# Storing the last tile of results in transfers of 64 rows in place of 32 rows

## The chip, the cores and the metric

The kernel runs on one core of one Trainium2 chip. The metric is the device time of one execution in microseconds (us), from the device's own record. Three runs of the kernel before gave 1005.03, 1005.83 and 1005.90 us, so the median is 1005.83 us and the runs lie within 0.9 us (0.09%) of each other.

A core has five engines that run side by side, each with an instruction queue of its own: PE multiplies matrices, DVE and ACT do elementwise work, POOL does too and issues transfers, and SP only issues transfers. Transfers between the on-chip memory (SBUF, 128 partitions) and the device memory (DRAM) are carried by 16 DMA engines, whichever queue issues them.

## The reference

The reference has two parts. The first is an attention without softmax: for each of 8 batches and 8 heads it forms the 64 by 64 matrix `kv` from `k` and `v`, multiplies `q` by it, and divides each row by its root mean square. The heads' results, side by side, are the 4608 by 512 input `x` of the second part, a gated feed-forward layer whose 4608 by 512 result is the output.

```python
kv = np.einsum('bhsd,bhse->bhde', k, v)
out = np.einsum('bhsd,bhde->bhse', q, kv)
rms = np.sqrt(np.mean(out * out, axis=-1, keepdims=True) + 1e-06)
x = (out / rms * g_norm).transpose(0, 2, 1, 3).reshape(B * S, H * D)    # 4608 x 512
...
gate = 1.0 / (1.0 + np.exp(-(x @ w_gate)))                              # 4608 x 1536
return gate * (x @ w_val) @ w_out                                       # 4608 x 512, float32
```

## The kernel before

The 4608 rows of `x` are worked through in 9 chunks of 512 rows (`c` from 0 to 8). A chunk goes through a first layer (gate and value) and a second layer (the product with `w_out`). From chunk 1 on both layers are computed with a recursive scheme of fewer block products: `first_layer_fast` makes 26 products for each of three parts, `second_layer_fast` makes 26 products over sums of blocks. The weight sums are kept in DRAM and loaded again for each chunk by POOL's queue. The attention of the next batches runs between the products.

The order of the work is written out by hand: every engine executes its instructions in the order in which the program issues them, and semaphores hold back an instruction until what it needs is there.

**The second layer's end.** `second_layer_fast(c, at)` runs the products in the order 0, 3, 1, 2, 6, 4, 5, 7 and on to 25. After each product `finish(i)` issues the elementwise steps that the product completes (`combine`, on DVE and ACT) and then the stores that have become possible. A chunk's result is four tiles `rows[t]` of 128 rows by 512 columns, each made of two halves of 256 columns. The table `dones` says after which product a tile is done: tile 0 after product 18, tile 1 after 22, tile 2 after 24, tile 3 after 25. In the last chunk (`c == NG - 1`, that is 8), tile 3 is stored in two halves: the second half, columns 256 to 511, after product 23, the first half, columns 0 to 255, after product 25, which is the last product of the kernel.

**The stores.** `store` writes one tile. From batch 1 on the rows of a chunk do not stand in the order of the output: row `(p, g, i)` of a batch's 576 output rows, with `p` of 32, `g` of 9 and `i` of 2, was worked on at place `i`, `g`, `p`. So 32 neighbouring partitions of a tile (`QB`) are 32 output rows which lie 18 rows apart, and the next 32 partitions are the next `g`, two output rows further on. The kernel before issues one transfer for each such group of 32 rows, four for a tile. Its pattern is 32 rows by 256 or 512 float32 on both sides. In the last chunk the transfers go alternately to SP's and ACT's queue (`ends`, line 1047), in the other chunks all to SP's.

The last three stores of the kernel therefore are: second half of tile 3 (four transfers of 32 rows by 1 KB, two on each queue), tile 2 (four of 32 rows by 2 KB), first half of tile 3 (four of 32 rows by 1 KB). After them the program waits until all transfers have landed and ends.

Of the kernel before, what the change touches and what calls it, by code (L numbers as in the profile page):

```python
# [20 lines left out]
def kernel(  # L21
# [11 lines left out]
    nc = tc.nc  # L33

    B, H, S, HD = q.shape
    T, DM = out.shape
# [14 lines left out]
    QB = 32  # L51
# [14 lines left out]
    NG = T // G  # L66
    NST = 3
    NF2 = NFT // 2
    DH = DM // 2
    NT = G // P  # L70
# [459 lines left out]
    def sg_tile():  # L530
        return sgs[next(sg_turns) % len(sgs)]

    def store(c, t, ot, cols=slice(0, DM), queues=(nc.sync,)):

        r0 = i = 0
        while r0 < P:
            b, s = divmod(G * c + P * t + r0, S)
            rows = out[S * b:S * b + S, cols]
            if b < NE // NHP:
                j, p = divmod(s, NP)  # L540
                n = min(P - r0, NP - p)
                queues[i % len(queues)].dma_start(out=rows.rearrange("(p j) d -> j p d", j=NJ)[j, p:p + n],
                                                  in_=ot[r0:r0 + n, cols])
            else:

                half, c0 = divmod(s, S // 2)
                n = QB
                queues[i % len(queues)].dma_start(
                    out=rows.rearrange("(p g i) d -> i g p d", p=QB, i=2)[half, c0 // QB],
                    in_=ot[r0:r0 + n, cols])  # L550
            r0 += n
            i += 1
# [15 lines left out]
    def at_ps():  # L568
        return psum.tile([P, NAT, 512], FP32, tag="at", name="at")
# [4 lines left out]
    def take():  # L574
        i = free.popleft()
        return i, bank(i)[:, 0:GH]
# [62 lines left out]
    for token in order.split():  # L639
        name = token.rstrip("0123456789.")  # L640
        n = [int(i) for i in token[len(name):].split(".")]
# [81 lines left out]
    def h_form(v, j):  # L723
        s_ = h_at[v]
        return h_main[j][:, s_] if s_ < 4 * NT else h_more[:, j, s_ - 4 * NT]
# [3 lines left out]
    def h_sums(j, some):  # L729
        ops = []  # L730
        for v, (x, sign, y) in list(SUMS.items())[some]:
            eng = nc.vector if j == N3 - 1 and v in ON_VECTOR else nc.gpsimd
            ops.append((eng, lambda v=v, x=x, sign=sign, y=y, eng=eng: eng.tensor_tensor(  # L733
                out=h_form(v, j), in0=h_form(x, j), in1=h_form(y, j), op=op_of(sign))))
        return ops
# [41 lines left out]
    def load_granule(g):  # L777
        if g < N_GRAN:
            n = 2 * P * len(PARTS[g % NPA])
            nc.gpsimd.dma_start(out=granule(g)[:, 0:n], in_=kept1[g // NPA % N3, g % NPA][:, 0:n])  # L780
# [35 lines left out]
    for some in places.split():  # L816
        p, names = some.split(":")
# [4 lines left out]
    for f in range(1, NFT):  # L822
        if f == NFT - 1:
            last = at_ps()
# [86 lines left out]
    def combine(o, regions, steps, mult):  # L911

        o.update({r: v[1] for r, v in regions.items()})
        for step in steps.split():
            if step[0] == "s":
                nc.scalar.activation(out=o["o" + step[1]], in_=o["o" + step[1]], func=AF.Sigmoid)  # L916
            elif "*" in step:
                x, y = step.split("*")
                mult.tensor_tensor(out=o[x], in0=o[x], in1=o[y], op=ALU.mult)  # L919
            else:  # L920
                out_, expr = step.split("=")
                if expr in regions:
                    nc.scalar.copy(out=o[out_], in_=o[expr])  # L923
                else:
                    sign = "+" if "+" in expr else "-"
                    x, y = expr.split(sign)
                    tt(out=o[out_], in0=o[x], in1=o[y], op=ALU.add if sign == "+" else ALU.subtract)  # L927

    def give_all(regions, last, i):
        for r in list(regions):  # L930
            if i == last[r]:
                give(regions.pop(r)[0])
# [60 lines left out]
    def w_raw(v):  # L993
        n, l = divmod(v, 4)
        b0 = block(l, 0)
        return w2[:, b0:b0 + NF2 - 1:2, DH * n:DH * n + DH]
# [12 lines left out]
    def ring(i):  # L1009
        i %= NR  # L1010
        return places[i]

    def load_w(i):
        if i < N_FAST * NS:
            nc.gpsimd.dma_start(out=ring(i), in_=kept3[i % NS].rearrange("p (j n) -> p j n", j=N3))
# [24 lines left out]
    def second_layer_fast(c, at):  # L1040
        o = {f"t{n}": temps[:, i, 0:DH] for i, n in enumerate((0, 1, 8, 9))}
        rows = [sg_tile() for _ in range(NT)]
        for t in range(NT):
            for n in range(2):
                o[f"o{2 * t + n}"] = rows[t][:, DH * n:DH * n + DH]
        regions, used, done = {}, {}, count()
        ends = (nc.sync, nc.scalar) if c == NG - 1 else (nc.sync,)
        first_loads = {9: 0, 10: 1, 13: 2, 23: 3}
        dones = {18: 0, 22: 1, 24: 2, 25: 3}

        def product(i, js):
            name, hv, wv, _ = PRODUCTS2[i]
            if i not in used:
                used[i] = name not in regions
                if used[i]:
                    regions[name] = take()
            ws = W_AT[wv] if c == 1 else w_raw(wv) if wv < 8 else stay[wv] if wv in STAY else ring((c - 2) * NS + STREAM.index(wv))
            for j in js:
                nc.tensor.matmul(regions[name][1], h_form(hv, j), ws[:, j], start=(used[i] and j == 0),  # L1059
                                 stop=(j == N3 - 1), skip_group_check=True)  # L1060

        def finish(i):
            _, _, wv, steps = PRODUCTS2[i]
            combine(o, regions, steps, nc.gpsimd)
            give_all(regions, LAST2, i)
            if c > 1 and wv > 7 and wv not in STAY and STREAM.index(wv) + NR < NS:
                load_w((c - 2) * NS + STREAM.index(wv) + NR)
            if c == 1:
                if i in first_loads:
                    load_granule(first_loads[i])  # L1070
            elif i == 16:
                load_granule(NPA * N3 * (c - 1) + NPA - 1)
            if i in dones:
                t = dones[i]
                store(c, t, rows[t], slice(0, DH if c == NG - 1 and t == NT - 1 else DM), ends)
            elif c == NG - 1 and i == 23:
                store(c, NT - 1, rows[NT - 1], slice(DH, DM), ends)
            for step in at.get(next(done), ()):
                step()
            sums_of_h(2)  # L1080

        for j in (1, 2):
            h_fill.extend(h_sums(j, slice(SUMS_FIRST, None)))
        on_pool = deque(step for eng, step in h_fill if eng is nc.gpsimd)

        def sums_of_h(n):
            for _ in range(n):
                if on_pool:
                    on_pool.popleft()()

        sums_of_h(2)
        for eng, step in h_fill:
            if eng is nc.vector:
                step()
        h_fill.clear()
        blocks, some = range(N3), range(N3 - 1)
        product(0, blocks)
        finish(0)
        for i in (1, 2, 6):
            product(i, some)  # L1100
        product(3, blocks)
        finish(3)
        for i in range(1, NPR):
            if i != 3:
                if i in (1, 2, 6):
                    if i == 6:
                        continue
                    product(i, (N3 - 1,))
                    finish(i)
                    if i == 2:  # L1110
                        product(6, (N3 - 1,))
                        finish(6)
                else:
                    product(i, blocks)
                    finish(i)
        load_late(c + 2)

    fill.extend(x_early)
    for t in range(G // P):
        for f in range(NFT - 2, NFT):  # L1120
            second(t, f)
            slot()
        ot = sg_tile()
        nc.scalar.copy(out=ot, in_=ps[t])
        store(0, t, ot)
# [62 lines left out]
```

## Time and profile before

| what | value |
|---|---|
| median of three runs | 1005.83 us |
| the profiled execution's own time | 1004.44 us |
| its span, first to last instruction | 1002.7 us |
| PE busy | 993.8 us (99% of the span) |
| DVE, POOL, ACT busy | 722.1, 617.5, 342.5 us |
| last instruction of DVE, the last half tile | 998.77 to 999.19 us |
| granted TensorE clock | 1.00 |
| read from DRAM, written | 160.50 MB, 25.56 MB |

Times inside the profile are microseconds from the start of the span. The profiled execution took 1.39 us less than the median of the runs, and 1.74 us of its time lies outside its span. A transfer has two times: how long its issue holds the queue that issues it, and how long it takes from the start of the issue until all its data has landed. The profile also records the packets that the 16 DMA engines move; the DMA share of a stretch is the sum of the packets' times over 16 engines, so that one engine that is busy all the time is 0.06, and packets that overlap on an engine can bring it over 1.

### The profile page before, as it was taken

How to read it: one execution, taken by the hardware profiler on the slowest of the kernel's cores; microseconds unless marked ns; L12 is line 12 of the kernel's file. 1: busy time of each engine (PE TensorE's matmuls, PEld its weight loads, DVE VectorE, ACT ScalarE, POOL GpSimd, SP SyncE). 2: the span in 40 equal slices, each digit the busy share in tenths (PEclk: the TensorE clock that was granted, in tenths of full speed). 3: DMA queues.
4: the chain of work that ended last, by engine and by line, in shares of the span. 5: the costliest groups of instructions: out<-in, count | busy, mean ns of one | idle time of the engine just before them, and what ended most of it. 6: DMA issues, size and time to landing. Idle time of an engine off the chain costs nothing.

```text
span 1002.7 us, 16624 instructions
## 1 busy us (share of the span) xinstructions
PE 993.8 (99%) x5958; PEld 815.8 (81%) x5958; DVE 722.1 (72%) x1198; ACT 342.5 (34%) x606; POOL 617.5 (62%) x988
## 2 busy tenths in 40 slices
PE   8999999999999999999999999999999999999998
PEld 7455447888888888888888888888888888888887
DVE  4989999889757756784677676866587566755672
ACT  4566332562144213530344124421342133213320
POOL 1509997798359633965186707861595449744963
PEclk9999999999999999999999999999999999999999
DMA  9995414673799568846875577755864555444514
GB/s 271 269 265 183 172 51 115 215 236 127 248 301 272 176 189 240 239 156 203 257 240 171 181 223 237 203 171 179 258 201 141 167 173 211 156 149 162 214 53 122
DMA packets 156114, 195.43 MB, mean 195 GB/s; under 512 B 84832, under 2 KB 128864, under 8 KB 156032
## 3 DMA queue, kind: packets, MB, share of 16 engines
q0 software_dynamic: 22000, 114.11, 34.4%
q1 hardware_dynamic: 126864, 78.16, 27.6%
q10 hardware_dynamic: 7168, 2.10, 0.9%
q8 instruction: 47, 0.77, 0.3%
q14 instruction: 35, 0.29, 0.1%
HBM read 160.50 MB, written 25.56 MB: 186 GB/s over the span
## 4 chain that ended last, share of the span: by engine, by line
PE 73%; POOL 2%; DMA 1%; issue 0%; SPq 0%; DVE 0%; POOLq 0%
PE mm L957 46%; PE mm L1059 24%; PE at L439 1%; POOL h L733 1%; PE at L389 1%; DMA h_more<-in_v_dram 1%; POOL w_ring L1030 0%; POOL h_more L733 0%; PE at L396 0%; SPq L134 0%; POOL w L780 0%; DVE sg L927 0%; POOLq L780 0%; POOLq L1030 0%
## 5 line engine op out<-in xcount | busy, mean ns | idle before, releaser
L957 PE MATMUL mm<-xs,w 128*128 128x256 f32 x1428 | 331.8, 380 | 0.0
L957 PEld LDWEIGHTS mm<-xs,w 128*128 128x128 f32 x1428 | 270.5, 190 | 37.1
L957 PE MATMUL mm<-xT,w 128*128 128x256 f32 x948 | 229.8, 380 | 0.0
L957 PEld LDWEIGHTS mm<-xT,w 128*128 128x128 f32 x948 | 179.5, 190 | 25.0 <-issue 0.5
L780 POOL DMA_DIRECT2D w<-kept x84 | 46.8, 557 | 189.4 <-PE mm L957 187.3
L927 DVE TENSOR_TENSOR sg<-sg,mm 128x512 f32<-128x512 f32 (+1 forms) x176 | 100.7, 599 | 85.5 <-PE mm L957 41.5
L1059 PE MATMUL mm<-w,h 128*128 128x256 f32 x630 | 143.1, 379 | 0.3 <-POOL h L733 0.3
L1059 PEld LDWEIGHTS mm<-w,h 128*128 128x128 f32 x630 | 119.6, 190 | 17.0 <-POOL h L733 0.7
L919 POOL TENSOR_TENSOR h<-h,sg 128x512 f32<-128x512 f32 x72 | 96.0, 1350 | 57.0 <-DVE h L927 31.0
L923 ACT COPY temps<-mm 128x512 f32<-128x512 f32 (+1 forms) x128 | 66.0, 538 | 186.9 <-PE mm L1059 94.7
L733 POOL TENSOR_TENSOR h<-h 128x128 f32<-128x128 f32 x216 | 112.1, 531 | 16.6 <-DVE h_more L733 13.1
L1059 PE MATMUL mm<-w,h_more 128*128 128x256 f32 x474 | 108.2, 379 | 0.0
L916 ACT ACTIVATE sg<-sg 128x512 f32<-128x512 f32 x96 | 59.7, 630 | 131.5 <-DVE sg L927 131.5
L1059 PEld LDWEIGHTS mm<-w,h_more 128*128 128x128 f32 x474 | 90.1, 190 | 12.2
L923 ACT COPY sg<-mm 128x512 f32<-128x512 f32 (+1 forms) x112 | 56.9, 510 | 86.5 <-PE mm L1059 45.0
L733 POOL TENSOR_TENSOR h_more<-h 128x128 f32<-128x128 f32 x120 | 61.6, 517 | 34.3 <-DVE h L919 30.0
L927 DVE TENSOR_TENSOR temps<-temps,mm 128x512 f32<-128x512 f32 (+1 forms) x96 | 59.4, 619 | 25.9 <-PE mm L1059 16.6
L599 PE MATMUL mm<-xT,w 128*128 128x512 f32 x176 | 77.8, 596 | 0.1
L927 DVE TENSOR_TENSOR temps<-mm,temps 128x512 f32<-128x512 f32 (+1 forms) x64 | 39.8, 622 | 50.9 <-PE mm L1059 23.6
L923 ACT COPY h<-mm 128x512 f32<-128x512 f32 x48 | 28.1, 585 | 140.4 <-PE mm L957 126.4
L927 DVE TENSOR_TENSOR sg<-mm,sg 128x512 f32<-128x512 f32 (+1 forms) x64 | 39.7, 620 | 45.1 <-PE mm L957 24.5
L599 PEld LDWEIGHTS mm<-xT,w 128*128 128x128 f32 x176 | 32.6, 190 | 39.2 <-issue 36.8
(145 smaller groups left out, 1284.2 us busy)
## 6 DMA issues: line engine op xcount, KB each, us to landing
w<-kept POOLq DMA_DIRECT2D x42, 896.0 KB, 5.7
w<-kept POOLq DMA_DIRECT2D x90, 384.0 KB, 4.6
w<-kept POOLq DMA_DIRECT2D x42, 768.0 KB, 5.5
out_dram<-sg SPq DMA_DIRECT2D x119, 64.0 KB, 1.7
h_more<-in_k_dram SPq DMA_DIRECT2D x28, 256.0 KB, 5.6
h_more<-in_v_dram SPq DMA_DIRECT2D x28, 256.0 KB, 6.5
q<-in_q_dram SPq DMA_DIRECT2D x96, 72.0 KB, 5.0
xT<-xTs SPq DMA_DIRECT2D x96, 72.0 KB, 4.4
```

Source lines behind the costliest of these rows:

```text
L389: nc.tensor.matmul(ps[HD * g:HD * g + HD, m, e], mains[2 * m + g, "k"][:, c], mains[2 * m + g, "v"][:, c], start=(e == 0 and j == 0), stop ...
L439: nc.tensor.matmul(u[HD * e:HD * e + HD, o:o + HD], qTs[HD * g:HD * g + HD, c:c + HD], kvq[HD * g:HD * g + HD, t == NSL, m, e], start=True ...
L599: nc.tensor.matmul(self.ps[i], w[("wg", "wv")[i], self.f][:, m, :], xT[self.c][:, m, :], start=(m == 0), stop=(m == NMT - 1), skip_group_c ...
L733: ops.append((eng, lambda v=v, x=x, sign=sign, y=y, eng=eng: eng.tensor_tensor(out=h_form(v, j), in0=h_form(x, j), in1=h_form(y, j), op=op ...
L780: nc.gpsimd.dma_start(out=granule(g)[:, 0:n], in_=kept1[g // NPA % N3, g % NPA][:, 0:n])
L916: nc.scalar.activation(out=o["o" + step[1]], in_=o["o" + step[1]], func=AF.Sigmoid)
L919: mult.tensor_tensor(out=o[x], in0=o[x], in1=o[y], op=ALU.mult)
L923: nc.scalar.copy(out=o[out_], in_=o[expr])
L927: tt(out=o[out_], in0=o[x], in1=o[y], op=ALU.add if sign == "+" else ALU.subtract)
L957: nc.tensor.matmul(regions[name][1][:, g], ws[:, g], xf[c][wv], start=(new and g == 0), stop=True, skip_group_check=True)
L1059: nc.tensor.matmul(regions[name][1], h_form(hv, j), ws[:, j], start=(used[i] and j == 0), stop=(j == N3 - 1), skip_group_check=True)
```

## The change

`store` gets a parameter `n_groups`, the number of 32-row groups that one transfer covers. Both stores of the last chunk's tile 3 pass 2; every other store passes 1 or leaves the default of 1. With 2, a transfer takes 64 neighbouring partitions of the tile; on the DRAM side its pattern is `[half, g:g + 2]` of the same arrangement, that is 2 groups by 32 rows by 256 columns, where the groups lie two output rows apart and the rows of a group 18 rows apart. The two dimensions cannot be merged into one. Each half of tile 3 is stored in two transfers, the first on SP's queue and the second on ACT's.

```diff
-    def store(c, t, ot, cols=slice(0, DM), queues=(nc.sync,)):
+    def store(c, t, ot, cols=slice(0, DM), queues=(nc.sync,), n_groups=1):
...
                 half, c0 = divmod(s, S // 2)
-                n = QB
+                n = QB * n_groups
+                assert n_groups == 1 or c0 + n <= S // 2
+                g = c0 // QB
                 queues[i % len(queues)].dma_start(
-                    out=rows.rearrange("(p g i) d -> i g p d", p=QB, i=2)[half, c0 // QB],
+                    out=rows.rearrange("(p g i) d -> i g p d", p=QB, i=2)[half, g:g + n_groups],
                     in_=ot[r0:r0 + n, cols])
...
-                store(c, t, rows[t], slice(0, DH if c == NG - 1 and t == NT - 1 else DM), ends)
+                last = c == NG - 1 and t == NT - 1
+                store(c, t, rows[t], slice(0, DH if last else DM), ends, 2 if last else 1)
             elif c == NG - 1 and i == 23:
-                store(c, NT - 1, rows[NT - 1], slice(DH, DM), ends)
+                store(c, NT - 1, rows[NT - 1], slice(DH, DM), ends, 2)
```

## The prediction

> **What bounds the kernel now.** I read the page first, for the engine that fills the span, then the chain that ended last, for what comes after that engine's last instruction, then the rows of the last stores, then stretches of DMA traffic, for the price of a packet.
>
> The page (busy time by engine; below it the chain that ended last):
>
> ```profile
> PE 993.8 (99%) x5958; PEld 815.8 (81%) x5958; DVE 722.1 (72%) x1198; ACT 342.5 (34%) x606; POOL 617.5 (62%) x988
> ...
> PE 73%; POOL 2%; DMA 1%; issue 0%; SPq 0%; DVE 0%; POOLq 0%
> ```
>
> PE is the bound until its last product. The change touches no instruction of PE, DVE or POOL, so only what follows that product can move. The chain in order of time, its end (start us, us, what):
>
> ```profile
> 965.06 33.69 PE mm L1059 x156
> 998.74 0.02 issue
> 998.77 0.42 DVE sg L927
> ```
>
> DVE finishes the last half tile at 999.19. The span ends at 1002.66, so a tail of 3.47 us is all that a better store could ever shorten. What fills it: the transfers still in flight, the first line below from the waits of SP's queue, the others from the issues of the stretch from 985 us on (KB each, median us from issue to landing):
>
> ```profile
> SPq L1183 <- DMA out_dram<-sg: 1.2, 1, 1.2
> ...
> out_dram<-sg ACTq DMA_DIRECT2D x6, 64.0 KB, 2.0
> out_dram<-sg SPq DMA_DIRECT2D x6, 64.0 KB, 1.8
> out_dram<-sg SPq DMA_DIRECT2D x4, 32.0 KB, 1.5
> out_dram<-sg ACTq DMA_DIRECT2D x4, 32.0 KB, 1.8
> ```
>
> The second of the two issues on each queue, in the rows of the store's line (duration ns, start us; below, time to landing):
>
> ```profile
> L548 SPq DMA_DIRECT2D out_dram<-sg x1: 495/495/495, 999.6 to 999.6; - x1
> L548 ACTq DMA_DIRECT2D out_dram<-sg x1: 442/442/442, 999.6 to 999.6; - x1
> ...
> DMA to landing us min/median/max: 1.7/1.8/1.8
> ```
>
> The first issues start at 999.22 and hold SP for 0.315 and ACT for 0.375 us; the second follow about 0.4 us later, and ACT's lands at about 1001.5. From there 1.2 us of semaphores close the program. So the tail is 0.4 us for a second issue, 1.8 us of transfer, 1.2 us of closing.
>
> DMA traffic in four stretches (us, the engines' busy time, granted clock, DMA share, GB/s; the last two columns matter):
>
> ```profile
> 84.00:86.00 2.00, 2.00 (x6) 0.82 (x5) 2.00 (x3) 0.44 (x1) 2.00 (x2) 1.00 1.07 372
> 999.90:1000.03 0.13, 0.00 (x0) 0.00 (x0) 0.00 (x0) 0.00 (x0) 0.00 (x0) 1.00 0.18 32
> 1000.03:1000.34 0.31, 0.00 (x0) 0.00 (x0) 0.00 (x0) 0.00 (x0) 0.00 (x0) 1.00 0.78 182
> 1000.00:1002.00 2.00, 0.00 (x0) 0.00 (x0) 0.00 (x0) 0.00 (x0) 0.00 (x0) 1.00 0.29 66
> ```
>
> From 84 to 86 us all traffic is packets of 1 KB (742 packets, 0.74 MB) with all engines full: 372 / 16 = 23.3 GB/s for one engine, 44 ns for 1 KB. In the tail it is 66 / (0.29 x 16) = 14.2 GB/s while busy, 72 ns for 1 KB. Data of the last store begins at 1000.03, 0.81 us after its issue, and its two first transfers, 64 packets of 1 KB, are through most of the engines 0.3 us later; one engine alone would need 64 x 44 ns = 2.8 us. So a transfer of 32 rows is spread over many engines.
>
> **The change, part by part.**
>
> *Fewer issues.* Four stores of tile 3 go from eight issues to four. On each queue the second issue of the last store falls away: the last data is asked for at 999.22 instead of 999.6, a gain of up to 0.4 us. The same issues gone after product 23 (997.4) gain nothing: the store of tile 2 behind them waits for DVE, whose step ends at 997.89, when SP and ACT are nearly free as it is (tile 2's issues start at 997.98 and 998.04; at most 0.1 us earlier).
>
> *A costlier issue.* The new transfer has a third dimension. SP's transfers of three dimensions at line 473 hold the queue for 595 ns (median) against 315 for the 32-row store. I take 0.2 us more until its data starts; bounds 0 (the issue is pipelined) and 0.3.
>
> *How the data is dealt out.* Each new transfer is 64 packets of 1 KB. This decides the sum, and no row shows it: every store of the kernel before begins with 32 rows or more on both sides, and those are spread over many engines. The new one begins with 2 on the DRAM side (2 groups by 32 rows by 256). If the work is cut along the outermost dimension, as fits all rows of before, it falls into two pieces, one for each of two engines, 32 packets each. If both dimensions are cut together, 16 engines get four packets each. I take two engines: the pattern's outer dimension has only two pieces to give, and the two cannot be merged since their steps are 2 and 18 rows.
>
> The Trainium skill, "DMA: Bandwidth & Descriptors", section "Why a DMA increments its semaphore by 16 and not by 1", states this rule: the engines used are the largest number up to 16 that divides both patterns' outermost sizes larger than one, and from SP and ACT they are the lowest-numbered. By it 64 and 2 give two engines, the same two for both queues, and the sum is the one below; no run of before has such a transfer.
>
> *The sum with two engines, both queues on the same two.* The half tile after product 23 is issued at 997.09; its data starts at 997.09 + 0.81 + 0.2 = 998.1. Each of the two engines has from it 32 packets from SP and 32 from ACT. Tile 2 adds two packets of 2 KB per transfer and engine, eight in all: from 999.10 to 999.30 the traffic is 205 GB/s at a share of 0.91, 14.1 GB/s and 145 ns a packet; I take 1.0 us for the eight. The last half tile, wanted from 1000.25 on, adds 64 more packets and finds the queue of its engines not yet empty: 64 x 47 ns = 3.0 us, plus tile 2, lasts until about 1002. So the two engines work without a pause from 998.1: 128 x 47 ns + 1.0 = 7.0 us, until 1005.1. Before, the last data was through at about 1001.1 (landing at 1001.5). The end moves by +4.0 us, the saved issue being contained in it. The price of 47 ns lies near the lower row (44 ns) because 14 engines are idle meanwhile; the upper row is 72 ns, which gives 9.2 + 1.2 us, until 1008.5, +7.4 us. From below: if the first half were through before the second begins, 1000.25 + 64 x 44 ns = 1003.1, +2.0 us. The closing 1.2 us is taken as unchanged.
>
> *Who waits.* Nobody but the program's end: after DVE's last step no engine has work, no tile is used again, and tile 2's own packets are delayed on two engines only, ending before the last half tile does.
>
> *Against which time.* The profiled execution took 1004.44 us and would take 1008.4. The runs' median stands 1.39 us higher; I add the change to it: 1005.83 + 4.0 = 1009.8 us, +0.40%.
>
> **The rivals.**
>
> *Sixteen engines, not slower.* The data is spread as before, four packets an engine per transfer. SP: 999.22 + 0.2 + 1.5 + two packets more at 72 ns = 1001.1; ACT 0.2 later, 1001.3 against 1001.5. Time 1005.83 - 0.2 = 1005.6, no change that can be measured (0.2%, 2 us, is about what a measurement can tell here). It speaks for it that nothing in the trace is ever confined to a few engines; against, that no transfer there begins with so small a dimension. It decides if landing of the new transfers stays under about 3.5 us.
>
> The Trainium skill's same page, section "Rules for kernel authors", advises merging many small transfers into one large one, since under 64 KB one pays mostly overhead. That speaks for the change; the rows here (32 KB in 1.5 us, 64 KB in 1.8) agree that size costs little, but by them it is worth 0.4 us at most.
>
> *Two engines, but a different pair for each queue.* Each engine then has 32 packets a store: 998.1 + 1.5 is over before 1000.25, and the last store's data ends at 1000.25 + 32 x 47 ns = 1001.8, or 1001.9 with what is left of tile 2: +0.8 us, 1006.6. Nothing in the profile tells engines apart by queue.
>
> *A real gain.* To be faster by 2 us the tail of 3.5 us would have to shrink to 1.5 us, of which 1.2 is closing. Only the runs' spread of 0.9 us could feign a gain.
>
> **How the numbers follow.** Two shared engines 0.84; sixteen 0.10; two separate pairs 0.04; anything else 0.02. The predicted time is the first's, 1009.8. Its bounds, +2.0 and +7.4, are 1007.8 and 1013.2; widened a little by the runs' spread, 1007.4 to 1013.4, which holds nearly all of the 0.84 and leaves out the two rivals, 0.14. Slower by over 0.2%: 0.84; within 0.2%: 0.14; faster: 0.02.
>
> **What would show it.** Right: the four transfers of tile 3 land about 4 to 5 us (first half stored) and 6 us (last) after issue instead of 1.5 to 1.8; from about 1000.5 to 1005 the DMA share stands near 2/16 = 0.13 with some 43 GB/s; SP's wait for the last landing grows from 1.2 to over 5 us; PE and DVE end where they do now. Wrong: the share stays above 0.5 for a fraction of a microsecond after 1000.2 and landing stays near 1.8 (sixteen engines); or it lasts half as long at twice the share (separate pairs). A packet price of 72 ns rather than 47 shows as 28 GB/s at the same share.

## The result and the profile after

The changed kernel takes 1009.80 us (median of five runs, 1009.43 to 1010.74) against 1005.23 us for the kernel before (five runs, 1004.59 to 1005.90): a ratio of 1.0047, 95% interval 1.0036 to 1.0058. It is slower by about 4.6 us, with 3.6 to 5.8 us in the interval.

The page after, busy time by engine, and the end of the chain that ended last (start us, us, what):

```profile
span 1008.9 us, 16620 instructions
...
PE 993.6 (98%) x5958; PEld 815.6 (81%) x5958; DVE 721.0 (71%) x1198; ACT 342.5 (34%) x606; POOL 618.3 (61%) x988
```

```profile
966.25 33.68 PE mm L1061 x156
999.93 0.02 issue
999.95 0.42 DVE sg L929
```

PE, DVE and ACT work no longer than before, POOL 0.8 us longer in 618. The span is 6.2 us longer, but DVE's last step ends 1.2 us later already, at 1000.37 instead of 999.19. That part is not the change's. The two chains are 1.2 us apart already at 284 us, long before the first changed store, behind a load from DRAM (first the line before, then the line after):

```profile
283.44 1.12 PE at L389 x30
284.63 1.12 PE at L389 x30
```

Over the nine profiles of this study DVE's end lies anywhere from 998.8 to 1002.2 us, in kernels that issue the same work up to there, 999.16 and 1002.23 among kernels with merged stores. So the profiles are compared by the **tail**, from the end of DVE's last step to the end of the span: 3.47 us before, 8.57 us after, +5.1 us.

The tail after, in the waits of SP's queue and in the issues from 996 us on (KB each, median us to landing; this view gives no landing for the half tiles):

```profile
SPq L1186 <- DMA out_dram<-sg: 6.6, 3, 3.2
...
out_dram<-sg SPq DMA_DIRECT2D x6, 64.0 KB, 4.3
out_dram<-sg ACTq DMA_DIRECT2D x6, 64.0 KB, 4.4
```

SP waits 6.6 us for stores at the end, against 1.2 before. The issues themselves, first those of the half tile after product 23, then those of the last one (duration ns, start us):

```profile
L550 SPq DMA_DIRECT2D out_dram<-sg x1: 650/650/650, 998.3 to 998.3; - x1
L550 ACTq DMA_DIRECT2D out_dram<-sg x1: 1362/1362/1362, 998.3 to 998.3; - x1
```

```profile
L550 SPq DMA_DIRECT2D out_dram<-sg x1: 560/560/560, 1000.4 to 1000.4; - x1
L550 ACTq DMA_DIRECT2D out_dram<-sg x1: 549/549/549, 1000.6 to 1000.6; - x1
```

There is one issue less on each queue, and those that remain are longer. What follows them, in stretches (the last two columns are the DMA share and GB/s):

```profile
1000.40:1001.70 1.30, 0.00 (x0) 0.00 (x0) 0.00 (x0) 0.00 (x0) 0.00 (x0) 1.00 0.61 53
1001.80:1002.80 1.00, 0.00 (x0) 0.00 (x0) 0.00 (x0) 0.00 (x0) 0.00 (x0) 1.00 0.84 229
1005.40:1007.00 1.60, 0.00 (x0) 0.00 (x0) 0.00 (x0) 0.00 (x0) 0.00 (x0) 0.50 0.13 47
1007.50:1008.90 1.40, 0.00 (x0) 0.00 (x0) 0.00 (x0) 0.00 (x0) 0.00 (x0) 0.50 0.00 0
```

and, in the kernel before, the stretch of its last half tile:

```profile
999.90:1001.10 1.20, 0.00 (x0) 0.00 (x0) 0.00 (x0) 0.00 (x0) 0.00 (x0) 1.00 0.50 113
```

The third line is the reading that matters: long after the last issue the traffic is steady at 47 GB/s with a share of 0.13, which is two of sixteen engines (2/16 = 0.125). Each moves 23.5 GB/s, one packet of 1 KB in 44 ns. Before, the share was 0.50 and the rate 113 GB/s. Both queues are at work in the third line: the packets of SP's last transfer run until 1007.10, those of ACT's from 1004.74 to 1007.45. Two separate pairs of engines would give a share of 0.25 there. (PE has no work left in these stretches, so its granted clock bears on nothing.) The fourth line is the closing, with no traffic.

### The profile page after: what moved, and what is told of

The parts are those of the page before. It is cut to its first block, busy times and chain, and to the rows that moved or that the text cites. A ratio compares the mean times of both kernels' runs of the same rounds, so it can differ in the third digit from the quotient of the medians.

```text
span 1008.9 us, 16620 instructions
## 1 busy us (share of the span) xinstructions
PE 993.6 (98%) x5958; PEld 815.6 (81%) x5958; DVE 721.0 (71%) x1198; ACT 342.5 (34%) x606; POOL 618.3 (61%) x988
## 4 chain that ended last, share of the span: by engine, by line
PE 73%; POOL 2%; DMA 1%; issue 0%; DVE 0%; POOLq 0%
PE mm L959 46%; PE mm L1061 24%; PE at L439 1%; POOL h L735 1%; PE at L389 1%; DMA h_more<-in_v_dram 1%; POOL w_ring L1032 0%; POOL h_more L735 0%; PE at L396 0%; POOL w L782 0%; DVE sg L929 0%; POOLq L782 0%; POOLq L1032 0%
```

## The experiments

The theory was that of the prediction: the pattern's outermost dimension says on how many engines a transfer runs; with 2 groups that is two, the same two for both queues. Rival A was that 64 rows or a third dimension make a transfer slow in itself, whatever the engines; rival B that the store after product 23 does the harm by what it holds up. All tails are the span less the end of DVE's last step, each from its own profile, one for each kernel:

| kernel | half after product 23 | last half | tail us | against before us | ratio (95% interval) |
|---|---|---|---|---|---|
| before | 4 x 32 rows | 4 x 32 rows | 3.47 | | |
| the change | 2 x 64 | 2 x 64 | 8.57 | +5.10 | 1.0047 (1.0036 to 1.0058) |
| last_only | 4 x 32 | 2 x 64 | 6.27 | +2.80 | 1.0037 (1.0023 to 1.0052) |
| first_only | 2 x 64 | 4 x 32 | 5.84 | +2.37 | 1.0029 (1.0018 to 1.0041) |
| four_groups | 1 x 128, on SP | 1 x 128, on SP | 4.55 | +1.08 | 1.0015 (1.0003 to 1.0026) |
| one_step | 2 x 64, one step | 2 x 64, one step | 3.42 | -0.05 | 0.9993 (0.9982 to 1.0003) |
| two_by_16 | 4 x (2 by 16) | 4 x (2 by 16) | 8.04 | +4.57 | 1.0048 (1.0033 to 1.0062) |
| last_one_queue | 4 x 32 | 2 x 64, both on SP | 6.11 | +2.64 | 1.0022 (1.0011 to 1.0033) |
| last_one_narrow | 4 x 32 | 1 x 64 on SP, 2 x 32 on ACT | 4.51 | +1.04 | 1.0014 (0.9999 to 1.0028) |

### The same 64 rows with another outermost dimension

```diff
-                    out=rows.rearrange("(p g i) d -> i g p d", p=QB, i=2)[half, g:g + n_groups],
+                    out=side[(c0 // QB) // 2 - 2, :, cols] if n_groups == 2 else rows.rearrange("(p g i) d -> i g p d", p=QB, i=2)[half, g],
...
+    side = kept_pool.tile([2, PH, 18 * DM], FP32, name="side")
```

> Both halves of tile 3 go out in two transfers of 64 rows each as in the change, on the same two queues, but to a side buffer in DRAM whose 64 rows lie one step of 36 KB apart, so that the DRAM side has an outermost dimension of 64 and no third one. The last 128 rows of the output are left unwritten. Theory (outermost dimension): all 16 engines, four packets of 1 KB on each for a transfer, no loss: a tail of 3.2 to 3.5 us, -0.2 us to 0 against before. Rival A in the form of 64 rows or a transfer of 64 KB being slow in itself: a tail near 8.5 us, +4.5 us.

The tail is 3.42 us, from a span of 1002.58 us and this last piece of its chain:

```profile
998.74 0.42 DVE sg L930
```

That is no loss, with the same number of transfers, rows and bytes on the same queues as in the change. The data of the last half tile in this kernel (same columns):

```profile
1000.30:1000.80 0.50, 0.00 (x0) 0.00 (x0) 0.00 (x0) 0.00 (x0) 0.00 (x0) 1.00 0.85 197
```

A share of 0.85 is as much work as 13 or 14 engines do without a pause, not two. Rival A's first form, that 64 rows in a transfer are slow, falls. The run also prices what merging would be worth if it kept the engines: nothing that shows. One issue less on each queue saves 0.4 us, but the 64-row issue holds SP for 0.494 us instead of 0.315 and its first data comes 1.15 us after the issue instead of 0.81, so ACT's last landing is 2.27 us after DVE's end, against 2.29 before.

### The same 32 rows with an outermost dimension of 2

```diff
-                n = QB * n_groups
-                assert n_groups == 1 or c0 + n <= S // 2
-                g = c0 // QB
+                n = QB
+                g, p0 = (5 + 2 * (i // 2), 16 * (i % 2)) if n_groups == 2 else (c0 // QB, 0)
...
-                    out=rows.rearrange("(p g i) d -> i g p d", p=QB, i=2)[half, g:g + n_groups],
+                    out=rows.rearrange("(p g i) d -> i g p d", p=QB, i=2)[half, g:g + n_groups, p0:p0 + QB // n_groups],
```

> Eight transfers of 32 rows and 32 KB as before, in the same order on the same queues, but each with a DRAM pattern of 2 groups by 16 rows by 256 columns (all 128 rows of the tile are written, in another order among themselves). Theory (outermost dimension): two engines for each of them, in all the same 128 packets of 1 KB on each of the two as in the change: a tail of 8 to 9 us, +4 to +5.5 us, although no transfer is larger than before. Rival A in the form of rows or size: no loss, a tail of 3.5 to 4 us; in the form of the third dimension's issue alone (0.6 against 0.35 us, two issues a queue): +0.5 us, a tail of 4 us.

A tail of 8.04 us, within the theory's 8 to 9, from a span of 1006.81 us and this end of the chain:

```profile
998.34 0.42 DVE sg L928
```

The transfers are as small and as many as before; only the pattern differs, and nearly the whole loss is there. Its late traffic:

```profile
1003.20:1005.50 2.30, 0.00 (x0) 0.00 (x0) 0.00 (x0) 0.00 (x0) 0.00 (x0) 0.50 0.13 45
```

The same two engines' worth. With this Rival A falls in its size form; in the form of a costly third dimension it would have given a tail of 4 us. Part of the 8.04 us passes through a wait: the last issue on each queue uses the semaphore of an earlier narrow transfer and starts when that has landed, at 1000.76 on SP's and 1002.50 on ACT's queue. It is the narrow transfers that are late there too.

### Four groups in one transfer

```diff
-                store(c, t, rows[t], slice(0, DH if last else DM), ends, 2 if last else 1)
+                store(c, t, rows[t], slice(0, DH if last else DM), ends, 4 if last else 1)
...
-                store(c, NT - 1, rows[NT - 1], slice(DH, DM), ends, 2)
+                store(c, NT - 1, rows[NT - 1], slice(DH, DM), ends, 4)
```

> Both halves of tile 3 go out in one transfer of 128 rows each, 4 groups by 32 rows by 256 columns, on SP's queue alone. Theory (outermost dimension): four engines, 32 packets of 1 KB on each for a half, 32 x 42 ns = 1.4 us; the half after product 23 is through before the last half begins, whose data runs from 1.2 us after its issue for 1.4 us: a tail of 0.03 + 1.2 + 1.4 + 0.4 + 1.1 = 4.1 us, +0.6 us against before, 4 us less than with two groups, though the transfers are twice as large. Rival A (third dimension or size): transfers of twice the rows are as slow or slower than those of 64, a tail of 8 us or more.

The tail is 4.55 us, 0.45 more than expected, and 4 us less than with two groups although every transfer is twice as large. The last half tile:

```profile
1003.80:1005.20 1.40, 0.00 (x0) 0.00 (x0) 0.00 (x0) 0.00 (x0) 0.00 (x0) 0.66 0.28 95
```

Twice the share and twice the rate of the two-group kernel: four engines at 23.8 GB/s each. The engines can also be counted. Every transfer ends in packets of 4 bytes, and each 32-row transfer of the kernel before has 16 of them (SP's queue has 9552 for its 597 transfers). That it is one for each engine used is inferred, but the counts fit the shares. The last half tile, first before (four transfers end in the stretch from 1000.10 to 1001.10), then in the change (two, 1004.10 to 1007.50), with four groups (one, 1004.00 to 1005.30) and with one step (two, 1000.30 to 1001.10); the number to read is that of packets under 512 B:

```profile
DMA packets 183, 0.12 MB, mean 122 GB/s; under 512 B 64, under 2 KB 183, under 8 KB 183
DMA packets 127, 0.13 MB, mean 37 GB/s; under 512 B 4, under 2 KB 127, under 8 KB 127
DMA packets 117, 0.12 MB, mean 89 GB/s; under 512 B 4, under 2 KB 117, under 8 KB 117
DMA packets 160, 0.13 MB, mean 164 GB/s; under 512 B 32, under 2 KB 160, under 8 KB 160
```

For one transfer that is 16, 2, 4 and 16. So 2, 4 and 64 groups or rows in front gave two, four and all sixteen engines. The Trainium skill's rule ("DMA: Bandwidth & Descriptors", section "Why a DMA increments its semaphore by 16 and not by 1"), the largest number up to 16 that divides both patterns' outermost sizes, gives 2, 4 and 16 for these three; the shares of 0.13, 0.28 and 0.85 and these counts agree. Of the 0.45 us, 0.36 are the start of the data, 1.56 us after the issue where I had taken 1.2. Packets of tile 2 were still under way then (until 1003.95); that they held it up is inferred.

### Which of the two stores costs what

Only the last half merged:

```diff
-                store(c, NT - 1, rows[NT - 1], slice(DH, DM), ends, 2)
+                store(c, NT - 1, rows[NT - 1], slice(DH, DM), ends, 1)
```

> Only the last half of tile 3 (after product 25) goes out in two transfers of 64 rows; the half after product 23 goes out in four of 32 as before. The tail is the time from the end of DVE's last step to the end of the span: 3.47 us before, 8.5 us with the whole change. Theory (a transfer is dealt out along the outermost dimension of its pattern, here 2, so it runs on two engines, the same two for both queues): the engines are free when the last half comes, data begins about 1.2 us after the issue, 64 packets of 1 KB on each engine at 42 to 44 ns take 2.7 us, then 0.4 us to landing and 1.1 us of closing: a tail of 5.5 us, +2.0 us against before. Rival A (it is the transfer itself that is slow, its third dimension or its 64 rows, whatever the engines): the last transfers alone make nearly the whole loss, a tail of 7 to 8.5 us. Rival B (the narrow store after product 23 does all the harm by what it holds up): a tail of 3.3 to 3.6 us.

Only the half after product 23 merged:

```diff
-                store(c, t, rows[t], slice(0, DH if last else DM), ends, 2 if last else 1)
+                store(c, t, rows[t], slice(0, DH if last else DM), ends, 1)
```

> Only the half of tile 3 after product 23 goes out in two transfers of 64 rows; the last half goes out in four of 32 rows as before. The second transfer of the last half on each queue uses the semaphore of the 64-row transfer and is issued only when that has landed. Theory (two engines, and a wide transfer queued behind a narrow one waits for the narrow one's engines): tile 2's transfers land 3.5 to 4.6 us after issue instead of 1.8 to 2.0; by the trace of the whole change the 64-row transfers land 2.0 us (SP) and 3.4 us (ACT) after DVE's end, so the last transfer is issued at 3.4 and lands at 5.3: a tail of 6.2 to 6.6 us, +2.9 us against before. Rival (a narrow transfer occupies its two engines only and wide ones pass it): tile 2's transfers land within 2.5 us of their issue; the tail is the same 6 us or so by the semaphore alone.

The two runs cost +2.80 and +2.37 us. Rival B falls, since the last half alone makes over half of the loss. That the two add up to 5.17 us, near the 5.10 for both at once, is in part chance: first_only has a wait that the change does not have. Its last half has a second issue on each queue, which starts only when the 64-row transfer with the same semaphore has landed, on ACT's queue 3.34 us after DVE's end:

```profile
L550 ACTq DMA_DIRECT2D out_dram<-sg x1: 321/321/321, 1003.0 to 1003.0; - x1
```

The transfer then lands 1.46 us later, and 1.03 us of closing make the tail of 5.84. So this run shows what a narrow store does to those behind it; it does not price the change's first store alone. In neither run did the number come out as written: the last half gave 6.27 us where the theory said 5.5 (the next section is on that), the first gave 5.84 where it said 6.2 to 6.6, having taken 1.9 us for the 1.46. In the kernel with only the first half merged, the stores of tile 2 (duration ns, start us; time to landing):

```profile
L550 SPq DMA_DIRECT2D out_dram<-sg x2: 328/400/471, 998.4 to 998.8; - x2
...
DMA to landing us min/median/max: 4.2/4.4/4.5
```

Tile 2's transfers are those of the kernel before, where they landed after 1.8 to 2.0 us; here they take 4.2 to 4.5. So a store that runs on all engines and stands behind a narrow one waits for the narrow one's engines, as the theory had it: it is complete only when its share on the two busy engines is. The packets show this share: of tile 2's 64 on each queue, 56 have started by 1001.68 (SP) and 1002.10 (ACT), and the last 8, as many as two engines carry, start from 1002.04 and 1002.71 on.

### Why the last half alone cost 0.8 us more than the theory said

In that kernel the 64 packets of SP's transfer took 2.4 us (1.27 to 3.68 us after DVE's end), 75 ns for a packet and engine, and ACT's, which came when they were nearly through, 1.5 us, 47 ns. Two more runs were to tell whether two narrow transfers issued at once disturb each other, or whether the first one is slow by itself. Both transfers on SP's queue:

```diff
-                store(c, t, rows[t], slice(0, DH if last else DM), ends, 2 if last else 1)
+                store(c, t, rows[t], slice(0, DH if last else DM), (nc.sync,) if last else ends, 2 if last else 1)
```

> As the kernel in which only the last half goes out in two transfers of 64 rows (there a tail of 6.27 us; SP's data ran from 1.27 to 3.68 us after DVE's end, 75 ns a packet and engine, ACT's after it to 4.91 us, 47 ns), but both of them on SP's queue. Theory (two narrow transfers issued at once on two queues slow each other; alone a narrow one runs at 46 ns): the first one's data runs from 1.27 to 2.8, the second's follows to 4.3: a tail of 5.5 to 5.8 us. Rival (the first narrow transfer runs at 75 ns whatever stands beside it): the first to 3.7, the second to 5.1: a tail of 6.3 to 6.6 us.

And one 64-row transfer alone, beside two of 32 rows on ACT:

```diff
-                n = QB * n_groups
-                assert n_groups == 1 or c0 + n <= S // 2
+                n_here = n_groups if r0 == 0 else 1
+                n = QB * n_here
...
-                queues[i % len(queues)].dma_start(
-                    out=rows.rearrange("(p g i) d -> i g p d", p=QB, i=2)[half, g:g + n_groups],
+                (nc.scalar if n_groups > n_here else queues[i % len(queues)]).dma_start(
+                    out=rows.rearrange("(p g i) d -> i g p d", p=QB, i=2)[half, g:g + n_here],
```

> As the kernel in which only the last half goes out in two transfers of 64 rows, but only the first of them, on SP, is one of 64 rows; the other 64 rows go out on ACT in two of 32. Theory (alone a narrow transfer runs at 46 ns): data from 1.27 to 2.8 us after DVE's end, landing at 3.1: a tail of 4.1 to 4.4 us, +0.8 us against before. Rival (75 ns whatever stands beside it): data to 3.7, a tail of 5.1 us. Rival of the two engines (the rows are spread over 16): a tail of 3.5 us.

Neither side had it right. On one queue the data ran from 1.27 to 4.81 us and the tail is 6.11, between the two forecasts; alone it ran from 1.28 to 3.21, a tail of 4.51, again between. The stretches show what both had missed; first the two transfers on SP's queue, then the one alone:

```profile
1002.02:1002.62 0.60, 0.00 (x0) 0.00 (x0) 0.00 (x0) 0.00 (x0) 0.00 (x0) 1.00 0.12 14
1002.62:1003.20 0.58, 0.00 (x0) 0.00 (x0) 0.00 (x0) 0.00 (x0) 0.00 (x0) 1.00 0.14 48
1004.40:1005.50 1.10, 0.00 (x0) 0.00 (x0) 0.00 (x0) 0.00 (x0) 0.00 (x0) 0.54 0.14 48
```

```profile
1002.56:1003.90 1.34, 0.00 (x0) 0.00 (x0) 0.00 (x0) 0.00 (x0) 0.00 (x0) 0.84 0.13 45
```

Both engines are busy in all lines, but in the first 0.6 us they move 14 GB/s, eight packets of 55 to 254 ns where the rate of the second line would have moved 28; after that they run at 48 GB/s. The slow start comes with two narrow transfers on two queues, with two on one queue and with one alone, so it does not need a second one beside it: in the kernel with the last half on both queues the same stretch, from 1000.86 to 1001.45, shows a share of 0.12 and 16 GB/s. The transfer that follows does not have it: ACT's packets there take 46 ns from the first on. The slow start costs about 0.4 us. What is left of the 0.8 us are single stalled packets later on (up to 235 ns in the run on one queue, close to the place where the second transfer's data follows the first's). What holds these packets up the records don't tell; that stays open.

The second 32-row transfer on ACT, beside the narrow one, shows again who pays (duration ns, start us; time to landing):

```profile
L550 ACTq DMA_DIRECT2D out_dram<-sg x1: 432/432/432, 1001.1 to 1001.1; - x1
...
DMA to landing us min/median/max: 2.8/2.8/2.8
```

It landed after 2.8 us; the same transfer takes 1.84 in the kernel before. Of its 32 packets 28 have started by 1002.49; the last 4, two engines' share, run between SP's last ones, from 1003.35 to 1003.53. So a transfer on ACT's queue waits for the very engines that SP's narrow one uses.

## Why the prediction was right, and where a size was off

**The bound and its place.** Right: PE and DVE do the same work in the same time, and the whole difference that the change makes lies behind DVE's last step.

**How the data is dealt out.** Right, and it decides the sum: two engines, as share, rate and closing packets show (0.13 and 47 GB/s; 0.13 and some 43 were forecast, for 1000.5 to 1005; until about 1004 tile 2's packets cover it), and the same two for both queues, since otherwise the share would be twice that while both have packets under way. Which two of the sixteen they are the traces don't tell. The two runs that exchange the pattern (one_step, two_by_16) settle that it is not size, number of rows or number of transfers; four_groups, which has a third dimension as well and runs on four engines, settles that it is the outermost dimension and not the presence of a third. The rivals of sixteen engines and of two pairs fall with it.

**The sum.** 1009.8 us were forecast and 1009.80 measured, but part of this is chance: the forecast was added to a base of 1005.83 us, the median of the five runs is 1005.23, and the change cost as much more than forecast as the base came out lower. (The spread of 0.9 us in the first three runs was small too: in the rounds of the experiments 47 runs of the kernel before lie between 1003.27 and 1008.03 us.) The forecast of +4.0 us stands against +4.6 in the runs (interval 3.6 to 5.8) and +5.1 in the profiles' tails, from which its terms can be checked one by one:

- The start of the data: I took 0.81 + 0.2 = 1.0 us after the issue. It was 1.25 (issue at 998.27, first packet at 999.52): +0.25 us.
- The two engines' work: I took 7.0 us, 128 packets at 47 ns and 1.0 us for tile 2. It lasted from 999.52 to 1007.45, 7.9 us: +0.9 us. Two errors in it partly cancel. The two halves took 3.9 us (to 1003.45) and 3.5 us (from 1003.93) where 3.0 each were taken; tile 2's packets between them took 0.5 us and not 1.0. The price of a running packet was right and even high (44 ns), but the term lacks the slow starts, some 0.4 us in each half (14 GB/s in the first 0.5 us of the first, 19 GB/s in the first 0.6 us of the second), and the packets that stalled later.
- The closing: 1.2 us were taken; from the last landing seen by SP at 1007.81 to the end at 1008.95 it was 1.1. SP saw that landing 7.4 us after its last issue, where about 6 had been forecast.

Together 4.0 + 0.25 + 0.9 - 0.1 = 5.05, against 5.10.

**The issues.** "A costlier issue" was right for SP (0.65 and 0.56 us) and wrong for ACT after product 23: 1.36 us, with ACT's data only at 1001.79, when SP's was nearly through. Behind it on ACT's queue stood tile 2's store, which started 0.5 us later against DVE's end than before, and the last half's, issued 0.23 us after SP's. The tail need not show this, since the two engines still had other packets until 1004.04.

**Who waits.** I wrote that tile 2's packets are delayed on two engines only and end before the last half tile does. The end is right (landing by 1004.5, 3.3 us before the last). The first part is too small: from 1000.40 to 1001.70 the share is 0.61 at 53 GB/s, so packets occupied about ten engines while moving a third of what such a share moves elsewhere (0.84 and 229 GB/s just after). Tile 2's packets on the other engines were held too: 22 of the 64 on SP's queue took over 300 ns (up to 815), where in the kernel before none of tile 2's took over 195.

**The rival's gain.** For sixteen engines I had reckoned -0.2 us and for merging 0.4 us at most. The run with sixteen engines shows -0.05 us in the tail. The Trainium skill's advice to merge small transfers ("DMA: Bandwidth & Descriptors", section "Rules for kernel authors") found no gain here between 32 and 64 KB.

No run points to a version that beats the kernel before: the best merged store, with all engines, ties with it.

## What to carry to other kernels

Before merging transfers, look at the outermost dimension of the merged pattern on both sides: groups that cannot be merged into one step put a small number in front, and the transfer then runs on that many DMA engines (2 groups: 47 GB/s, 4 groups: 95 GB/s). At the end of a kernel nothing hides this, and wide transfers queued behind a narrow one land late as well. A merged store that keeps all engines saved nothing measurable (0.05 us in one tail, a ratio of 0.9982 to 1.0003 in the runs), so there was little to win by merging.

## What the runs showed of the hardware that was not expected

- A narrow transfer alone, or the first of two, starts slowly: 14 GB/s for its first 0.6 us, then 48 GB/s, on the same two engines. The cause is open.
- Of two narrow transfers issued within 5 ns of each other on two queues, ACT's issue lasted 1.36 us where SP's lasted 0.65, and its data came only when SP's was nearly through (2.3 us later in the changed kernel; 1.36 us and 2.1 to 2.2 us in last_only and first_only). Issued 0.23 us apart, the last half's two took 0.56 and 0.55 us. The cause was not tried.
- While narrow transfers were under way, packets of a wide one on other engines lasted several times as long as usual (a share of 0.61 at 53 GB/s). The cause wasn't tried.
